# The moving operand of the MLP matmuls, read in turn from two halves

## Chip, cores and metric

One core of one Trainium2 chip runs the whole program. The metric is the device time of one execution in microseconds (us). The kernel before took 1102.36 us (median of three runs, 1100.85 to 1103.11). The profile is of one further execution on the same kind of chip.

## What is computed

Inputs are q, k, v of shape (4, 8, 576, 64), a scalar tau, and four weight matrices that arrive as 8-byte floats. Three stages follow each other; the tokens are 4 x 576 = 2304 and the model width is 512.

```python
scores = q @ k.T / 8
keep   = scores >= max(scores) - tau            # the rest counts as -1e9
x      = softmax(scores over keep) @ v          # -> 2304 x 512
g1     = relu(x @ w1i) ** 2                     # 2304 x 2048
x2     = g1 @ w1o                               # 2304 x 512
h      = x2 @ w2i                               # 2304 x 2048
out    = (h * tanh(log1p(exp(min(h, 20))))) @ w2o
```

## The kernel before

The kernel does not issue its work in the order of its loops. Every piece of work is an `op` with the engines that may do it, a cost for each, and the buffers that it reads and writes. `Plan.order` then simulates the engines with those costs, and the instructions are issued in the order of the simulated starts. The costs are constants in the source: a group of twelve matmuls of an MLP product has `T: 1.41`, a group of six wide ones `T: 1.39`, readers of PSUM `A: 0.48` on ScalarE and `V: 0.6` or `0.66` on VectorE. There is no hand-written order of the MLP work beside this.

The MLP work is cut into nine blocks of 256 tokens. TensorE works on float32 data in its float32r form: each product is the sum of three matmuls, high x high, high x low and low x high, where high is the value as rounded to float32r and low the rest (`passes`).

- **Layer 1, up (`first_part`, `mlp_in`)**: for each of eight slices j of 256 hidden units, two halves f of 128; for each, four chunks c of the model width and three passes. The stationary operand is a 128 x 128 piece of the weights, the moving operand is `x` with 256 columns, one for each token of the block. So it is 24 matmuls of 256 columns for each j, into the PSUM tile `h`.
- **Layer 1, down (`down` in `first_part`)**: the stationary operand is a piece of `w1o`, the moving operand is the 256 tokens of `gh` or `gl`: 24 matmuls of 256 columns for each j, into `acc`.
- **Layer 2, up (`second`, `mlp_in`)**: as in layer 1, 16 groups of 12 matmuls with 256 columns for each block, into halves of `s0`, `s1`, `h` or `small`.
- **Layer 2, down (`down` in `second`)**: here the tokens are the stationary operand (128 of them) and the weights move, with 512 columns: 24 matmuls for each of the four quarters of a block, into `acc`.

Before the change each moving operand is one run of neighbouring 4-byte elements: `r(c)` in `mlp_in` and `z()[:, f, :]` in the two `down`. A piece of PSUM is read by `relu` (L1072) and `evac` (L1106) in layer 1, by `exp` (L1123), `add` (L1182), `gate` (L1195) and `evac` (L1217) in layer 2; each of these reads 512 neighbouring elements and writes 512 neighbouring elements to SBUF. All matmuls are issued by one helper, `mm`, at L379, and stand in the profile under that line. A row such as `h<-xh,wi0l` has the output first, then the moving and the stationary tile.

Attention for the first tokens runs alone; from about 140 us on the first MLP layer runs beside attention, and from about 690 us on the second layer runs by itself.

Of the kernel before, what the change touches and what calls it, by code (L numbers as in the profile page):

```python
# [11 lines left out]
F32 = mybir.dt.float32  # L12
# [292 lines left out]
def attention_moe_moe_kernel(ctx: ExitStack, tc: tile.TileContext, q, k, v, tau, w1i, w1o, w2i, w2o, out):  # L305
# [688 lines left out]
    def mlp_in(layer, j, f, ph, col, x, due):  # L994
        wi = W[layer, 0, j]

        def fn(e):
# [5 lines left out]
        op({"T": 1.41}, fn, r=[wi[0], wi[1], *x[0].bufs, *x[1].bufs],  # L1003
           w=[ph.buf if isinstance(ph, Half) else ph], due=due)

    class View:


# [2 lines left out]

        def __call__(self, c):
            n = 4 // len(self.bufs)
            return self.bufs[c // n]()[:, c % n, :]

    def x_first(n, due):
        xh, xo = sbuf("xh", [128, 4, 256], F32R), sbuf("xo", [128, 4, 256], F32R)
        o = pbuf(rot("s0", "s1"), [128, 1024])
        for t in range(2):
            for g in range(2):  # L1020
                xl = sbuf(rot("xl0", "xl1", "xl2"), [128, 256], F32)
                dma(lambda e, xl=xl, t=t, g=g: e.dma_start(out=xl(), in_=x_dr[n]()[:, t, 256 * g:256 * g + 256]),
                    r=[x_dr[n]], w=[xl], due=due - 4, mb=0.13)

                def turn(e, o=o, xl=xl, z=512 * t + 256 * g):
                    for c in (0, 128):
                        nc.tensor.transpose(o()[:, z + c:z + c + 128], xl()[:, c:c + 128], ident)  # L1027

                op({"T": 0.17}, turn, r=[xl, K], w=[o], due=due - 0.5)

            def part(y, t=t):
                return y()[:, :, 128 * t:128 * t + 128]

            def src(o=o, t=t):
                return o()[:, 512 * t:512 * t + 512].rearrange("p (c n) -> p c n", c=4)

            def hi(e, src=src, part=part):
                if e == "A":
                    nc.scalar.activation(out=part(xh), in_=src(), func=AF.Copy)
                else:  # L1040
                    nc.vector.tensor_copy(out=part(xh), in_=src())

            def lo(e, src=src, part=part):
                nc.vector.tensor_tensor(out=part(xo), in0=src(), in1=f32(part(xh)), op=ALU.subtract)

            op({"A": 0.52, "V": 0.6}, hi, r=[o], w=[xh], due=due - 0.4 - URG)
            op({"V": 0.6}, lo, r=[o, xh], w=[xo], due=due - 0.3 - URG)
        return View([xh]), View([xo])

    def flat(t):  # L1050
        return t().rearrange("p f n -> p (f n)")

    def first(n):
        lent.discard("acc")
# [6 lines left out]
    def first_part(n, j, x, acc):  # L1061
        d = due_f(n, j)
        ph = pbuf("h", [128, 512])
        for f in range(2):
            mlp_in(0, j, f, ph, 256 * f, x, d + 0.1 * f)
        gh, gl = (sbuf(rot(f"{a}0", f"{a}1"), [128, 2, 256], F32R) for a in ("gh", "gl"))

        r = sbuf("r", [128, 512], F32)

        def relu(e, ph=ph, r=r):  # L1070
            if e == "A":
                nc.scalar.activation(out=r(), in_=ph(), func=AF.Relu)  # L1072
            else:
                nc.vector.tensor_scalar(out=r(), in0=ph(), scalar1=0.0, scalar2=None, op0=ALU.max)

        def square(e, r=r):
            if e == "A":
                nc.scalar.activation(out=r(), in_=r(), func=AF.Square)  # L1078
            else:
                VEC[e].tensor_tensor(out=r(), in0=r(), in1=r(), op=ALU.mult)  # L1080

        op({"A": 0.48, "V": 0.66}, relu, r=[ph], w=[r], due=d + 0.3 - URG + O_RELU)
        op({"A": 0.52, "P": 1.04, "V": 0.6}, square, x=[r], due=d + 0.4 + O_SQ, two=True)
        to_hi(r, gh, flat, d + 0.5 + O_SQ)
        to_lo(r, gh, gl, flat, d + 0.6 + O_SQ)
        wo = W[0, 1, j]
        for f in range(2):
            def down(e, j=j, f=f, wo=wo, gh=gh, gl=gl, acc=acc):
                for dt in range(4):
                    a = acc[0]()[:, 256 * dt:256 * dt + 256]  # L1090
                    for i, (l, z) in enumerate(passes(wo, (gh, gl))):
                        mm(a, l()[:, f, 128 * dt:128 * dt + 128], z()[:, f, :],
                           j == 0 and f == 0 and dt % 2 == 0 and i == 0,
                           j == 7 and f == 1 and dt % 2 == 1 and i == 2)

            first_ = j == 0 and f == 0
            op({"T": 1.41}, down, r=[wo[0], wo[1], gh, gl], w=acc if first_ else (),
               x=() if first_ else acc, due=d + 5.5 + O_DN + 0.1 * f)
        if j == NJ - 1:
            for h in range(2):  # L1100
                st = sbuf(rot("stg0", "stg1"), [128, 512], F32)

                def evac(e, h=h, st=st, acc=acc):
                    a = acc[0]()[:, 512 * h:512 * h + 512]
                    if e == "A":
                        nc.scalar.activation(out=st(), in_=a, func=AF.Copy)  # L1106
                    else:
                        nc.vector.tensor_copy(out=st(), in_=a)

                op({"A": 0.48, "V": 0.66}, evac, r=acc, w=[st], due=due_f(n, 7) + 6)  # L1110
                dma(lambda e, n=n, h=h, st=st: e.dma_start(out=x2_dr[n][h](), in_=st()),
                    r=[st], w=[x2_dr[n][h]], due=due_f(n, 7) + 7, mb=0.26)

    def second():
# [10 lines left out]
        for i, n in enumerate((*range(NB - 2), NB - 1, NB - 2)):  # L1125
# [1 line left out]
            hs, os_ = [], []  # L1127
            sets = (("f0", "f1", "e1", "nat0"), ("nat1", "KT0", "KT1", "V0"))[i % 2]
            for g in range(2):
                xr = sbuf(rot("V1", "hl0"), [128, 2, 256], F32)  # L1130
                dma(lambda e, n=n, g=g, xr=xr: e.dma_start(
                    out=xr().rearrange("p c n -> p (c n)"), in_=x2_dr[n][g]()),
                    r=[x2_dr[n][g]], w=[xr], due=blkd - 12, mb=0.26)
                xh, xo = sbuf(sets[2 * g], [128, 2, 256], F32R), sbuf(sets[2 * g + 1], [128, 2, 256], F32R)

                def flat2(t):
                    return t().rearrange("p c n -> p (c n)")

                def hi(e, xr=xr, xh=xh):
                    if e == "A":  # L1140
                        nc.scalar.activation(out=xh(), in_=xr(), func=AF.Copy)
                    elif e == "P":
                        nc.gpsimd.tensor_scalar(out=xh(), in0=xr(), scalar1=1.0, scalar2=0.0, op0=ALU.mult, op1=ALU.add)
                    else:
                        nc.vector.tensor_copy(out=xh(), in_=xr())

                def lo(e, xr=xr, xh=xh, xo=xo):
                    VEC[e].tensor_tensor(out=xo(), in0=xr(), in1=f32(xh()), op=ALU.subtract)

                op({"A": 0.52, "V": 0.34, "P": 0.66}, hi, r=[xr], w=[xh], due=blkd - 6, two=True)  # L1150
                op({"V": 0.6, "P": 1.24}, lo, r=[xr, xh], w=[xo], due=blkd - 5, two=True)
                hs.append(xh)
                os_.append(xo)
            x = View(hs), View(os_)
            acc = [pbuf("acc", [128, 1024])]
            for qd in range(4):
# [3 lines left out]
                    mlp_in(1, 2 * qd + f // 2, f % 2, ph[f // 2], 256 * (f % 2), x, d + 0.1 * f)  # L1160
                es = [sbuf(rot("pt2", "hl1", "f2", "Q0", "Q1"), [128, 512], F32) for _ in range(2)]
                gs = [sbuf(rot("r", "e0"), [128, 512], F32) for _ in range(2)]
                ghs = [sbuf(rot("gh0", "gh1", "pt0"), [128, 2, 256], F32R) for _ in range(2)]
                gls = [sbuf(rot("gl0", "gl1", "pt1"), [128, 2, 256], F32R) for _ in range(2)]
                for z in range(2):
                    def exp(e, z=z, ph=ph, ex=es[z]):
                        act(AF.Exp, "ln", ex(), ph[z]())

                    def cap(e, ex=es[z]):
                        nc.vector.tensor_scalar(out=ex(), in0=ex(), scalar1=E20, scalar2=None, op0=ALU.min)  # L1170
# [9 lines left out]
                for z in range(2):  # L1180
                    def add(e, z=z, ph=ph, ex=es[z]):
                        nc.vector.scalar_tensor_tensor(  # L1182
                            out=ex(), in0=ph[z](), scalar=20.0, in1=ex(), op0=ALU.min, op1=ALU.add
                        )

                    op({"V": 0.6}, add, r=[ph[z].buf], x=[es[z]], due=d + 0.8)
# [5 lines left out]
                op({"A": 1.04}, sig, x=es, due=d + 0.9, tab=("sig",))  # L1192
                for z in range(2):
                    def gate(e, z=z, ph=ph, ex=es[z], g=gs[z]):
                        nc.vector.tensor_tensor(out=g(), in0=ph[z](), in1=ex(), op=ALU.mult)  # L1195

                    op({"V": 0.6}, gate, r=[ph[z].buf, es[z]], w=[gs[z]], due=d + 1.0)
                    to_hi(gs[z], ghs[z], flat, d + 1.1)
# [1 line left out]
                for f in range(4):  # L1200
# [3 lines left out]
                    def down(e, f=f, qd=qd, wo=wo, g2=g2, acc=acc):  # L1204
                        for t in range(2):
                            for i, (z, l) in enumerate(passes(wo, g2)):
                                mm(acc[0]()[:, 512 * t:512 * t + 512], l()[:, f % 2, 128 * t:128 * t + 128], z()[:, f % 2, :],
                                   qd == 0 and f == 0 and i == 0, qd == 3 and f == 3 and i == 2)

                    first_ = qd == 0 and f == 0  # L1210
# [2 lines left out]
            ob = sbuf(rot("xh", "xo"), [128, 2, 512], F32)  # L1213
            for t in range(2):
                def evac(e, t=t, ob=ob, acc=acc):
                    if e == "A":
                        nc.scalar.activation(out=ob()[:, t, :], in_=acc[0]()[:, 512 * t:512 * t + 512], func=AF.Copy)  # L1217
                    else:
                        nc.vector.tensor_copy(out=ob()[:, t, :], in_=acc[0]()[:, 512 * t:512 * t + 512])

                op({"A": 0.48, "V": 0.66}, evac, r=acc, w=[ob], due=blk[NB + i + 1] + 6)

# [96 lines left out]
```

## Time and profile before

| what | value |
|---|---|
| time, median of three runs | 1102.36 us |
| span of the profiled execution | 1101.5 us |
| granted TensorE clock, mean over the span | 0.982 |
| instructions | 23735 |
| matmuls / weight loads in the trace | 9364 / 9364 |

The span is the time from the first to the last instruction of the profiled execution; it lies 0.9 us under the median of the runs. TensorE has two rows: PE, its matmuls, and PEld, its weight loads, which run beside the matmuls. Matmuls overlap each other, so the time that one costs in a dense stream is the distance from its start to the start of the next, not the duration in its row. [...]

### The profile page before, as it was taken

Reading aid. Unit: us, or ns where it says so; the run is one execution under the profiler, and the core shown is the slowest. Engines: PE = TensorE matmul, PEld = TensorE weight load, DVE = VectorE, ACT = ScalarE, POOL = GpSimd, SP = SyncE. Lnnn points to the kernel's source line nnn. Section 1 sums busy time; section 2 is a strip of 40 time slices with the busy share of each in tenths; the row PEclk is TensorE's granted clock in tenths of the full one; section 3 lists DMA queues with packets and bytes.
Section 4 is the critical chain, followed back from the end, with each engine's and each line's share of the span. In section 5 each row is a group of like instructions: output and inputs, shape, how many; then the busy total and the mean of one; then the engine's idle time right before and its main releaser. Section 6 shows DMA issues by size and latency. Waiting matters only on the chain.

```text
span 1101.5 us, 23735 instructions
## 1 busy us (share of the span) xinstructions
PE 1058.0 (96%) x9364; PEld 946.4 (86%) x9364; DVE 745.8 (68%) x1768; ACT 787.4 (71%) x1309; POOL 39.8 (4%) x38
## 2 busy tenths in 40 slices
PE   6788899899999999999999999999999999999998
PEld 4566598788898888898999999998899889989896
DVE  5889999999888998769664149854544445443352
ACT  6789798777777778667575369967766667676584
POOL 1231012000000000000000000000000000000000
PEclk9898889999999999999999999999999999999999
DMA  9535447888968988875664024310100101000000
GB/s 258 165 116 148 127 112 154 158 171 164 178 125 156 169 163 161 153 148 110 140 228 142 20 78 153 116 40 20 39 20 20 39 1 39 21 20 20 1 20 20
DMA packets 246416, 113.75 MB, mean 103 GB/s; under 512 B 211104, under 2 KB 228000, under 8 KB 246304
## 3 DMA queue, kind: packets, MB, share of 16 engines
q1 hardware_dynamic: 246016, 111.71, 43.8%
q8 instruction: 73, 1.20, 0.4%
q10 hardware_dynamic: 288, 0.52, 0.1%
q14 instruction: 39, 0.32, 0.1%
HBM read 58.33 MB, written 14.16 MB: 66 GB/s over the span
## 4 chain that ended last, share of the span: by engine, by line
PE 68%; DVE 6%; DMA 5%; ACT 2%; issue 2%; SPq 1%; DVEq 0%; ACTq 0%
PE acc L379 31%; PE h L379 16%; PE s L379 14%; PE small L379 6%; DMA pt<-hl 3%; DMA pt<-area 2%; DVE e L777 1%; DVE area L743 1%; DVE hl L806 1%; DVE area L806 1%; DMA area<-in_q_dram 1%; PE s L1027 0%; ACT e L766 0%; ACT area L801 0%; ACT hl L801 0%
## 5 line engine op out<-in xcount | busy, mean ns | idle before, releaser
L379 PE MATMUL s<-KT,area 64*128 64x64 f16 (+6 forms) x880 | 89.9, 327 | 4.8 <-ACT area L684 2.5
L508 DVE TENSOR_TENSOR gl<-r,gh 128x512 fp32r<-128x512 f32 x87 | 60.0, 690 | 47.7 <-ACT gh L498 46.2
L766 ACT ACTIVATE e<-area,m 128x576 f32<-128x576 f32 x100 | 75.6, 768 | 22.3 <-DVE area L743 9.5
L1119 ACT ACT_TABLE_LOAD x70 | 89.8, 1283 | 1.2
L743 DVE TENSOR_SCALAR_CACHE_REDUCE area<-s,c 128x576 f32<-128x576 f32 x100 | 79.5, 812 | 12.1 <-PE s L379 11.4
L777 DVE SCALAR_TENSOR_TENSOR e<-area,n,e 128x576 f32<-128x576 f32 x100 | 80.1, 813 | 5.5 <-ACT e L766 4.3
L1072 ACT ACTIVATE r<-h 128x512 f32<-128x512 f32 x72 | 42.8, 595 | 44.9 <-PE h L379 40.0
L806 DVE TENSOR_TENSOR hl<-e,hl 128x512 f16<-128x512 f32 (+1 forms) x142 | 64.5, 466 | 14.3 <-ACT hl L801 14.0
L498 ACT ACTIVATE gh<-r 128x512 fp32r<-128x512 f32 x90 | 56.6, 629 | 22.1 <-PE acc L379 19.9
L379 PE MATMUL small<-V,pt 128*128 128x64 f16 (+1 forms) x1680 | 64.1, 195 | 4.6 <-DMA pt<-hl 2.4
L1170 DVE TENSOR_SCALAR area<-area 128x512 f32<-128x512 f32 x37 | 15.8, 426 | 77.9 <-ACT area L1123 77.8
L379 PEld LDWEIGHTS <-pt 128*128 128x128 f16 (+1 forms) x1680 | 54.7, 101 | 15.2 <-issue 6.9
L801 ACT ACTIVATE hl<-e 128x576 f16<-128x576 f32 x74 | 50.2, 680 | 22.4 <-DMA pt<-hl 10.6
L508 DVE TENSOR_TENSOR gl<-e,gh 128x512 fp32r<-128x512 f32 x36 | 24.8, 690 | 39.8 <-ACT gh L498 39.7
L1123 ACT ACTIVATE area<-s 128x512 f32<-128x512 f32 x24 | 14.3, 598 | 46.1 <-PE s L379 46.1
L498 ACT ACTIVATE gh<-e 128x512 fp32r<-128x512 f32 x36 | 22.6, 629 | 33.7 <-PE acc L379 33.6
L1123 ACT ACTIVATE area<-area 128x512 f32<-128x512 f32 x74 | 46.3, 630 | 0.5
L1078 ACT ACTIVATE r<-r 128x512 f32<-128x512 f32 x72 | 45.3, 629 | 1.2
L379 PEld LDWEIGHTS <-area 64*128 64x128 f16 (+1 forms) x720 | 23.5, 97 | 21.0 <-issue 1.8
L379 PEld LDWEIGHTS s<-KT,area 64*128 64x128 f32 (+1 forms) x160 | 19.5, 209 | 19.4 <-issue 10.8
L806 DVE TENSOR_TENSOR area<-e,area 128x512 f16<-128x512 f32 (+1 forms) x67 | 30.5, 460 | 5.7 <-ACT area L801 5.7
L1195 DVE TENSOR_TENSOR r<-s,area 128x512 f32<-128x512 f32 x23 | 15.9, 691 | 27.1 <-ACT area L1123 27.1
(755 smaller groups left out, 4062.9 us busy)
## 6 DMA issues: line engine op xcount, KB each, us to landing
area<-in_moe_w_in_dram SPq DMA_DIRECT2D x22, 512.0 KB, 4.1
area<-in_moe_w_out_dram SPq DMA_DIRECT2D x22, 512.0 KB, 4.1
xl<-xdr SPq DMA_DIRECT2D x36, 128.0 KB, 2.6
x2dr<-stg SPq DMA_DIRECT2D x18, 256.0 KB, 4.0
xdr<-xs SPq DMA_DIRECT2D x32, 128.0 KB, 2.3
f<-in_v_dram SPq DMA_DIRECT2D x12, 256.0 KB, 3.0
f<-in_k_dram SPq DMA_DIRECT2D x22, 128.0 KB, 3.1
area<-in_q_dram SPq DMA_DIRECT2D x20, 128.0 KB, 2.8
```

The costliest lines, as they stand in the source:

```text
L379: nc.tensor.matmul(o, l, r, start=start, stop=stop, skip_group_check=True)
L498: nc.scalar.activation(out=o, in_=i, func=AF.Copy)
L508: VEC[e].tensor_tensor(out=part(lo), in0=src(), in1=f32(part(hi)), op=ALU.subtract)
L743: nc.vector.tensor_scalar(out=sc(), in0=s()[:, 0:576], scalar1=c()[:, 3:4], scalar2=None, op0=ALU.mult, op1=ALU.min, accum_out=m()[:, i:i ...
L766: lambda e: nc.scalar.activation(out=ex(), in_=sc(), func=AF.Exp, bias=m()[:, i:i + 1], scale=-1.0),
L777: nc.vector.scalar_tensor_tensor(out=ex(), in0=sc(), scalar=nt()[:, i:i + 1], in1=ex(), op0=ALU.is_le, op1=ALU.mult, accum_out=l()[:, 0, u ...
L801: nc.scalar.activation(out=hl()[:, 0:576], in_=ex(), func=AF.Copy)
L806: VEC[e].tensor_tensor(out=hl()[:, a:a + n], in0=ex()[:, z:z + n], in1=hl()[:, z:z + n], op=ALU.subtract)
L1072: nc.scalar.activation(out=r(), in_=ph(), func=AF.Relu)
L1078: nc.scalar.activation(out=r(), in_=r(), func=AF.Square)
L1119: nc.scalar.preload_act_table_set({"ln": "natural_log_exp_and_others", "sig": "sigmoid_and_others"}[table])
L1123: nc.scalar.activation(out=out, in_=in_, func=func, **kw)
```

## The change

Each tile that is a moving operand gets another order of its elements, or another order in which they are read. The tiles of tokens become two halves of 128 tokens, `[128, a, f, 128]` with a the half, instead of `[128, f, 256]`. A matmul then reads column 0 from half 0, column 0 from half 1, column 1 from half 0, and so on: neighbouring columns of the stream lie 2048 bytes apart (layer 1 up) or 1024 bytes apart (the other three products), and every second step goes back. For layer 2 down the weights keep their place, and their 512 columns are read in turn from two halves of 256 columns. The number of matmuls, their column counts and the PSUM places that they write stay as they are, and they write neighbouring columns of PSUM. Since the columns there are now mixed, the six readers of PSUM read every second element (a step of 8 bytes), first one half and then the other, and write neighbouring elements. The stationary operand of layer 2 down is still a run of 128 elements, taken at another offset. No cost and no parameter of the planner is changed, and no `op` is added or taken away.

```diff
+    def turned_out(t):
+        return t.rearrange("p (k a) -> p a k", a=2)
+
+    def halves(t):
+        return t.rearrange("p (a k) -> p a k", a=2)
...
         def __call__(self, c):
             n = 4 // len(self.bufs)
-            return self.bufs[c // n]()[:, c % n, :]
+            return self.bufs[c // n]()[:, :, c % n, :].rearrange("p a b -> p b a")
...
-        xh, xo = sbuf("xh", [128, 4, 256], F32R), sbuf("xo", [128, 4, 256], F32R)
+        xh, xo = sbuf("xh", [128, 2, 4, 128], F32R), sbuf("xo", [128, 2, 4, 128], F32R)
...
-                return y()[:, :, 128 * t:128 * t + 128]
+                return y()[:, t]
...
             if e == "A":
-                nc.scalar.activation(out=r(), in_=ph(), func=AF.Relu)
+                nc.scalar.activation(out=halves(r()), in_=turned_out(ph()), func=AF.Relu)
...
-                        mm(a, l()[:, f, 128 * dt:128 * dt + 128], z()[:, f, :],
+                        mm(a, l()[:, f, 128 * dt:128 * dt + 128], z()[:, :, f, :].rearrange("p a b -> p b a"),
...
-                    a = acc[0]()[:, 512 * h:512 * h + 512]
+                    a = turned_out(acc[0]()[:, 512 * h:512 * h + 512])
                     if e == "A":
-                        nc.scalar.activation(out=st(), in_=a, func=AF.Copy)
+                        nc.scalar.activation(out=halves(st()), in_=a, func=AF.Copy)
...
-                        act(AF.Exp, "ln", ex(), ph[z]())
+                        act(AF.Exp, "ln", halves(ex()), turned_out(ph[z]()))
...
-                            out=ex(), in0=ph[z](), scalar=20.0, in1=ex(), op0=ALU.min, op1=ALU.add
+                            out=halves(ex()), in0=turned_out(ph[z]()), scalar=20.0, in1=halves(ex()),
+                            op0=ALU.min, op1=ALU.add,
...
-                        nc.vector.tensor_tensor(out=g(), in0=ph[z](), in1=ex(), op=ALU.mult)
+                        nc.vector.tensor_tensor(
+                            out=halves(g()), in0=turned_out(ph[z]()), in1=halves(ex()), op=ALU.mult)
...
-                                mm(acc[0]()[:, 512 * t:512 * t + 512], l()[:, f % 2, 128 * t:128 * t + 128], z()[:, f % 2, :],
+                                mm(acc[0]()[:, 512 * t:512 * t + 512], l()[:, t, f % 2, :],
+                                   z()[:, f % 2, :].rearrange("p (a b) -> p b a", a=2),
...
+                    o, i = halves(ob()[:, t, :]), turned_out(acc[0]()[:, 512 * t:512 * t + 512])
                     if e == "A":
-                        nc.scalar.activation(out=ob()[:, t, :], in_=acc[0]()[:, 512 * t:512 * t + 512], func=AF.Copy)
+                        nc.scalar.activation(out=o, in_=i, func=AF.Copy)
```

## Rows read from the trace of the kernel before

**Rows 1.** Page, part 1: busy us (share of the span) and instructions of each engine.

```profile
PE 1058.0 (96%) x9364; PEld 946.4 (86%) x9364; DVE 745.8 (68%) x1768; ACT 787.4 (71%) x1309; POOL 39.8 (4%) x38
```

**Rows 2.** Windows: stretch, length, busy of PE, PEld, DVE, ACT, POOL, then clock, DMA share, GB/s.

```profile
0.00:212.65 212.65, 181.13 (x1550) 140.78 (x1552) 186.06 (x480) 174.88 (x326) 34.01 (x32) 0.91 0.60 154
212.65:300.00 87.35, 83.40 (x1052) 74.22 (x1049) 78.63 (x230) 65.86 (x115) 1.07 (x2) 1.00 0.87 171
300.00:500.00 200.00, 197.86 (x2388) 178.73 (x2385) 169.35 (x493) 145.22 (x250) 4.74 (x4) 1.00 0.81 151
500.00:700.00 200.00, 199.60 (x1866) 195.29 (x1866) 124.45 (x253) 129.34 (x223) 0.00 (x0) 1.00 0.47 130
700.00:1100.00 400.00, 396.05 (x2520) 357.34 (x2519) 187.27 (x317) 272.06 (x399) 0.00 (x0) 1.00 0.07 25
```

**Rows 3.** Waits of TensorE from 300 to 1095 us: total us, times, longest.

```profile
PE small L379 <- DMA pt<-hl: 1.6, 4, 0.6
PE h L379 <- DVE r L1195: 0.5, 1, 0.5
```

**Rows 4.** Waits of ScalarE from 300 to 1095 us: total us, times, longest.

```profile
ACT gh L498 <- PE acc L379: 52.3, 31, 4.7
ACT area L1123 <- PE s L379: 46.1, 15, 6.5
ACT r L1072 <- PE h L379: 38.5, 27, 4.2
```

**Rows 5.** Chain in order of time, 240 to 1101 us: start, us, what, matmuls in it.

```profile
731.51 11.30 PE s L379 x96
...
1033.48 11.17 PE acc L379 x48
```

**Rows 6.** Windows: one stretch in which nearly every matmul has 256 columns.

```profile
625.00:675.00 50.00, 50.00 (x423) 50.00 (x423) 27.02 (x46) 33.63 (x62) 0.00 (x0) 1.00 0.25 78
```

**Rows 7.** Timeline of TensorE, a quick stretch: start, duration; sixteen matmuls from first row to last.

```profile
600.06 0.28 PE L379 MATMUL h<-xo,wi1h 128*128 128x256 f32 x1
...
601.88 0.28 PE L379 MATMUL h<-xh,wi1l 128*128 128x256 f32 x1
```

**Rows 8.** Timeline of TensorE, a slow stretch: nine matmuls from first row to last.

```profile
630.25 0.28 PE L379 MATMUL acc<-gh,wo3h 128*128 128x256 f32 x1
...
631.34 0.28 PE L379 MATMUL acc<-gh,wo4h 128*128 128x256 f32 x1
```

**Rows 9.** Timeline of TensorE, scores in float16: from row to row 512 and 64 columns.

```profile
335.93 0.63 PE L379 MATMUL s<-KT,area 64*64 64x512 f16 x6
...
336.18 0.41 PE L379 MATMUL s<-KT,area 64*64 64x512 f16 x4
```

**Rows 10.** Windows: a stretch at the lower clock.

```profile
139.00:141.00 2.00, 2.00 (x11) 2.00 (x11) 2.00 (x5) 1.46 (x3) 1.97 (x2) 0.50 0.03 8
```

**Rows 11.** Timeline of TensorE in that stretch: six matmuls from first row to last.

```profile
139.17 0.41 PE L379 MATMUL h<-xo,wi0h 128*128 128x256 f32 x1
...
140.45 0.41 PE L379 MATMUL h<-xo,wi0h 128*128 128x256 f32 x1
```

**Rows 12.** Groups by form: count, then busy us, mean ns; idle before, and releaser.

```profile
L1072 ACT ACTIVATE r<-h 128x512 f32<-128x512 f32 x72 | 42.8, 595 | 44.9 <-PE h L379 40.0 <-DVE gl L508 3.8 <-DVE hl L806 0.7
L1078 ACT ACTIVATE r<-r 128x512 f32<-128x512 f32 x72 | 45.3, 629 | 1.2
L457 ACT ACTIVATE area<-area 128x512 int32<-128x512 uint32 x44 | 30.0, 681 | 0.0
L857 ACT ACTIVATE wo4l<-h 128x512 f32<-128x512 f32 x18 | 10.8, 601 | 1.1 <-PE small L379 1.1
L857 ACT ACTIVATE wo4l<-small 128x128 f32<-128x128 f32 x18 | 5.1, 283 | 0.4 <-PE small L907 0.4
L464 DVE SCALAR_TENSOR_TENSOR KT<-KT,area 128x512 int32<-128x512 int32 x10 | 6.9, 692 | 1.7 <-ACT area L457 1.4
L1182 DVE SCALAR_TENSOR_TENSOR area<-s,area 128x512 f32<-128x512 f32 x24 | 16.5, 688 | 7.1 <-ACT area L1123 7.0
```

More of the change, by code (lines that the diff above doesn't have):

```diff
@@ L1050, in flat @@
     def flat(t):
-        return t().rearrange("p f n -> p (f n)")
+        return t().rearrange("p a f b -> p (a f b)")
     def first(n):
@@ L1065, in first_part @@
             mlp_in(0, j, f, ph, 256 * f, x, d + 0.1 * f)
-        gh, gl = (sbuf(rot(f"{a}0", f"{a}1"), [128, 2, 256], F32R) for a in ("gh", "gl"))
+        gh, gl = (sbuf(rot(f"{a}0", f"{a}1"), [128, 2, 2, 128], F32R) for a in ("gh", "gl"))
         r = sbuf("r", [128, 512], F32)
@@ L1071, in relu @@
             if e == "A":
-                nc.scalar.activation(out=r(), in_=ph(), func=AF.Relu)
+                nc.scalar.activation(out=halves(r()), in_=turned_out(ph()), func=AF.Relu)
             else:
-                nc.vector.tensor_scalar(out=r(), in0=ph(), scalar1=0.0, scalar2=None, op0=ALU.max)
+                nc.vector.tensor_scalar(
+                    out=halves(r()), in0=turned_out(ph()), scalar1=0.0, scalar2=None, op0=ALU.max)
         def square(e, r=r):
@@ L1103, in evac @@
                 def evac(e, h=h, st=st, acc=acc):
-                    a = acc[0]()[:, 512 * h:512 * h + 512]
+                    a = turned_out(acc[0]()[:, 512 * h:512 * h + 512])
                     if e == "A":
-                        nc.scalar.activation(out=st(), in_=a, func=AF.Copy)
+                        nc.scalar.activation(out=halves(st()), in_=a, func=AF.Copy)
                     else:
-                        nc.vector.tensor_copy(out=st(), in_=a)
+                        nc.vector.tensor_copy(out=halves(st()), in_=a)
                 op({"A": 0.48, "V": 0.66}, evac, r=acc, w=[st], due=due_f(n, 7) + 6)
@@ L1129, in second @@
             for g in range(2):
-                xr = sbuf(rot("V1", "hl0"), [128, 2, 256], F32)
+                xr = sbuf(rot("V1", "hl0"), [128, 2, 2, 128], F32)
                 dma(lambda e, n=n, g=g, xr=xr: e.dma_start(
-                    out=xr().rearrange("p c n -> p (c n)"), in_=x2_dr[n][g]()),
+                    out=flat(xr), in_=x2_dr[n][g]()),
                     r=[x2_dr[n][g]], w=[xr], due=blkd - 12, mb=0.26)
-                xh, xo = sbuf(sets[2 * g], [128, 2, 256], F32R), sbuf(sets[2 * g + 1], [128, 2, 256], F32R)
-                def flat2(t):
-                    return t().rearrange("p c n -> p (c n)")
+                xh, xo = (sbuf(sets[2 * g + i], [128, 2, 2, 128], F32R) for i in range(2))
                 def hi(e, xr=xr, xh=xh):
@@ L1162, in second @@
                 gs = [sbuf(rot("r", "e0"), [128, 512], F32) for _ in range(2)]
-                ghs = [sbuf(rot("gh0", "gh1", "pt0"), [128, 2, 256], F32R) for _ in range(2)]
-                gls = [sbuf(rot("gl0", "gl1", "pt1"), [128, 2, 256], F32R) for _ in range(2)]
+                ghs = [sbuf(rot("gh0", "gh1", "pt0"), [128, 2, 2, 128], F32R) for _ in range(2)]
+                gls = [sbuf(rot("gl0", "gl1", "pt1"), [128, 2, 2, 128], F32R) for _ in range(2)]
                 for z in range(2):
                     def exp(e, z=z, ph=ph, ex=es[z]):
-                        act(AF.Exp, "ln", ex(), ph[z]())
+                        act(AF.Exp, "ln", halves(ex()), turned_out(ph[z]()))
                     def cap(e, ex=es[z]):
@@ L1215, in evac @@
                 def evac(e, t=t, ob=ob, acc=acc):
+                    o, i = halves(ob()[:, t, :]), turned_out(acc[0]()[:, 512 * t:512 * t + 512])
                     if e == "A":
-                        nc.scalar.activation(out=ob()[:, t, :], in_=acc[0]()[:, 512 * t:512 * t + 512], func=AF.Copy)
+                        nc.scalar.activation(out=o, in_=i, func=AF.Copy)
                     else:
-                        nc.vector.tensor_copy(out=ob()[:, t, :], in_=acc[0]()[:, 512 * t:512 * t + 512])
+                        nc.vector.tensor_copy(out=o, in_=i)
                 op({"A": 0.48, "V": 0.66}, evac, r=acc, w=[ob], due=blk[NB + i + 1] + 6)
```

## The prediction, made before the changed kernel ran

> **What bounds the kernel now.** I read the share of busy time first, then cut it into stretches, then looked at who waits for whom, and last at the distance between two matmuls. TensorE is busy for 96% of the span [rows 1], but that is a mean. By stretches it is 85% up to 212.65 us, 95% up to 300 us, and 99 to 100% after it, at clock 1.00, while VectorE goes from 85% down to 47% and ScalarE stays near 70% [rows 2]. From 300 us on the waits of TensorE are nothing: the longest sum is 1.6 us [rows 3]. The other way round ScalarE waits 52.3, 46.1 and 38.5 us for TensorE at three of its lines [rows 4]. So from 300 us to the end the time is the number of matmuls times the distance between their starts, and nothing but that distance can move it much.
>
> The distance is the thing to see. A stretch of the chain with 96 matmuls of 256 columns takes 11.30 us, 117.7 ns each; 48 of 512 columns take 11.17 us, 232.7 ns each [rows 5]. A stretch of the first layer gives 50.00 us / 423 = 118.2 ns [rows 6]. [...] It depends on which tiles meet: one stretch runs at (601.88 - 600.06) / 16 = 113.8 ns [rows 7], another at (631.34 - 630.25) / 9 = 121.1 ns [rows 8], of the same shape. [...]
>
> **The change part by part.** It adds and removes no instruction, no wait, no DMA and no planner cost, so the issue order of every queue stays. What changes is how long three kinds of instructions take.
>
> *Moving reads.* By the source there are 9 x 8 x 48 + 9 x 16 x 12 = 5184 matmuls of 256 columns and 9 x 4 x 24 = 864 of 512. The trace has no moving operand that jumps, so the new price is bounded from both sides. Low end: no loss, 106.7 and 213.3 ns, which saves 11.3 x 5184 = 58.6 us and 19 x 864 = 16.4 us, 75 us. High end: every column comes at the pace of the lower clock, 213.3 ns [rows 11] and twice that, which adds 95 x 5184 = 492 us and 194 x 864 = 168 us, 660 us. Nearest row for a stream whose supply is not the limit: float16, 0.434 ns a column [rows 9], that is 111.1 and 222.2 ns. I take that: two streams that are read in turn give each of them twice the time for its next piece, as half the bytes per column do. It saves 6.9 x 5184 = 35.8 us (from 118.0) and 9.8 x 864 = 8.5 us (from 232), 44.3 us. Not all of it counts. The first block of layer 1 lies before 212.65 us, where TensorE is idle for 15% [rows 2]; I give nothing for its 384 matmuls (2.6 us) and half for the next 384 (1.3 us). 44.3 - 3.9 = 40.4 us. The next limit is VectorE: from 212.65 to 500 us it is busy 248 of 287 us [rows 2], so a gain of 4% on TensorE (some 12 us there) still fits.
>
> [...]
>
> *Readers of PSUM.* 90 reads on ScalarE in layer 1 (72 `relu`, 18 `evac`, 595 ns each [rows 12]), and in layer 2 72 `exp`, 72 `add`, 72 `gate` and 18 `evac`. They now step by 8 bytes. Low end: nothing; on VectorE an operand in SBUF with that step (L464) takes 692 ns against 688 for neighbouring ones [rows 12]. High end: each element costs twice; 384 elements more cost 601 - 283 = 318 ns, 0.83 ns each, so 512 would cost 0.42 us more. Nearest row: the ScalarE read of SBUF with an 8-byte step, 681 ns against 629 [rows 12], 0.05 us. I take 0.05 us, about 9 us in all on ScalarE. Its cover is the waiting for TensorE [rows 4]. Even the high end, 90 x 0.42 = 38 us on ScalarE in each layer, fits under 272 of 400 us [rows 2] in layer 2, so I cost it at nothing; without the cover it would be those 9 us.
>
> *Writes of `xh`, `xo`, `gh`, `gl` and the stationary read at another offset.* Same element counts, still runs of 128 or more. Nothing either way.
>
> The sum: 1101.5 - 40.4 = 1061.1 us of span, and 0.9 us for the distance of the span to the median of the runs: 1062 us.
>
> **Rivals.**
>
> 1. *A smaller gain.* The loss stays as a floor and only the bad meetings of tiles go, so every matmul runs like the best stretch, 113.8 ns [rows 7], and 512 columns in the same ratio, 224 ns. It saves 4.2 x 5184 + 8.5 x 864 = 29 us, less 2.4 us for the first blocks: about 1075 us. For it: the 113.8 is steady over sixteen matmuls. This belongs to the forecast's case.
>
> [...]
>
> 3. *Somewhat slower.* The moving stream now touches two places at a time and meets the weight loads, which run beside it for 86% of the span [rows 1], more often. At the price of the bad stretch, 121.1 ns [rows 8], and 238 ns in the same ratio, it is 3.1 x 5184 + 6 x 864 = 21 us: 1123 us; twice as many meetings give 1144 us.
>
> 4. *It does not do what it says.* The loss has nothing to do with the order of the columns (it comes with float32r itself, or with the weight loads alone): 1102 us.
>
> **How the numbers follow.** Forecast and the smaller gain 0.55, rival 2 0.20, rival 3 0.13, rival 4 0.12. [...] The forecast's own range is 1034 us (no loss at all, 1102.4 - 68 with the first blocks taken out) to 1092 us (a quarter of the gain). The range that leaves out 2 in 10 goes from 1034 up to 1144 us, the upper price of rival 3, and leaves out rival 2 alone. Faster by over 0.2% (about what a measurement of this kernel can tell from no change): 0.55. Within 0.2%: 0.12. Slower: 0.33.
>
> **What would show it.** In the profile after: the distance between matmuls of 256 columns in the stretch of rows 6 and in the chain. Near 111 ns and the same in all stretches, the forecast is right; 113 to 114, the smaller gain; 118, rival 4; over 121, rival 3; near 213 at clock 1.00, rival 2. The 512-column matmuls should move in the same ratio, since the change treats them alike; if only one shape moves, the reason is the distance between the halves or the weight loads, and not the turn. ScalarE reads of PSUM near 0.65 us confirm the price of the step; near 1.0 us they would be the high end, still covered. If the distance falls and the time does not, the gain was lost between 212 and 500 us to VectorE. The prediction is wrong if the distance does not fall below 117 ns.

## The result and the profile after

The changed kernel takes 1072.73 us (median of four runs, 1072.09 to 1072.95) against 1102.41 us before: a ratio of 0.9737, 95% interval 0.9723 to 0.9751, 29.7 us less. The forecast was 1062 us, 40 us less. Its profiled execution has a span of 1070.3 us, 31.2 us under the span before.

The page's first part, against [rows 1]: TensorE loses 45 us of busy time; VectorE gains 3.6 us and ScalarE 7.8 us, though the change gives them no new work.

```profile
PE 1013.1 (95%) x9364; PEld 914.4 (85%) x9364; DVE 749.4 (70%) x1768; ACT 795.2 (74%) x1309; POOL 40.0 (4%) x38
```

The windows after, with the columns of [rows 2]:

```profile
0.00:212.65 212.65, 178.35 (x1591) 136.68 (x1592) 187.51 (x481) 177.65 (x327) 34.25 (x32) 0.94 0.62 154
212.65:300.00 87.35, 81.22 (x1018) 72.19 (x1017) 77.62 (x230) 64.72 (x114) 1.07 (x2) 0.98 0.91 170
300.00:500.00 200.00, 193.46 (x2402) 174.66 (x2399) 171.12 (x498) 145.25 (x249) 4.71 (x4) 1.00 0.85 153
500.00:700.00 200.00, 195.98 (x1917) 190.82 (x1915) 132.78 (x260) 142.99 (x235) 0.00 (x0) 1.00 0.49 131
700.00:1070.00 370.00, 364.09 (x2448) 340.03 (x2448) 180.33 (x304) 264.59 (x387) 0.00 (x0) 1.00 0.08 25
```

From 300 to 500 us TensorE now works 193.46 of 200 us, where it had 197.86, and issues 2402 matmuls there against 2388. It has become quicker and waits more; hardly any work was pulled forward.

The chain in order of time, against [rows 5]: a stretch of 256 columns and one of 512. 96 matmuls take 10.72 us, 111.7 ns each (117.7 before); 48 take 10.36 us, 215.8 ns each (232.7 before).

```profile
722.88 10.72 PE s L379 x96
...
1006.30 10.36 PE acc L379 x48
```

A stretch of the first layer, against [rows 6]: 35.00 us / 314 = 111.5 ns.

```profile
625.00:660.00 35.00, 35.00 (x314) 34.85 (x314) 20.39 (x34) 25.86 (x48) 0.00 (x0) 1.00 0.27 86
```

Taken over all pairs of neighbouring starts within a product, the 256-column matmuls are at 111.6 to 111.7 ns in all three products that have them, nearly all between 111 and 112, where before they lay between 112 and 125 with means of 117.9 to 118.7. The 512-column ones went from 232.1 to 215.9. What the read in turn removed is nearly all of the spread, and 6 to 7 ns of some 118 for 256 columns and 16.2 ns of 232.1 for 512.

Waits of TensorE from 290 to 1065 us, against [rows 3]: the transposes of the attention weights by DMA (`pt<-hl`) are waited for longest, 5.1 us against 1.6.

```profile
PE small L379 <- DMA pt<-hl: 5.1, 8, 1.2
PE h L379 <- DVE r L1200: 2.0, 1, 2.0
PE h L379 <- ACT r L1078: 1.5, 2, 0.8
```

The readers of PSUM with an 8-byte step, against [rows 12]: `relu` (L1072, now L1078) 594 ns where it took 595, `add` (L1182, now L1186) 686 against 688. The step cost nothing there. But a read that the change does not touch has become slower. The conversion of the weights on ScalarE reads SBUF with an 8-byte step (L457), 799 ns where it took 681; this line alone is 5.2 of ScalarE's 7.8 us.

```profile
L1078 ACT ACTIVATE r<-h 128x512 f32<-128x512 f32 x72 | 42.8, 594 | 36.7 <-PE h L379 30.2 <-DVE gl L508 5.7 <-DVE hl L464 0.8
L457 ACT ACTIVATE area<-area 128x512 int32<-128x512 uint32 x44 | 35.2, 799 | 0.0
...
L1186 DVE SCALAR_TENSOR_TENSOR area<-s,area 128x512 f32<-128x512 f32 x24 | 16.5, 686 | 6.8 <-ACT area L1130 6.8
```

Where the time came from is seen by three marks of TensorE's timeline: the first matmul of layer 1, the last group of attention's value products, and the first matmul of layer 2 into `h` (a first group of layer 2, into `small`, runs just before it).

```profile
134.99 0.58 PE L379 MATMUL h<-xh,wi0h 128*128 128x256 f32 x1 [1.66 <-ACT xh L1045]
...
550.08 1.48 PE L379 MATMUL small<-V,pt 128*128 128x64 f16 x42
...
678.88 0.49 PE L379 MATMUL h<-f,wi0h 128*128 128x256 f32 x2 [0.65 <-ACT r L1078]
```

The same marks in the runs that keep the order of the work, as lengths of the stages between them in us (from the timelines of one execution each; before has its marks at 137.30, 554.11 and 686.94):

| stage | before | after | layer 1 only | layer 2 only | before, light DMA | after, light DMA | after, light mask |
|---|---|---|---|---|---|---|---|
| attention alone | 137.3 | 135.0 | 132.2 | 131.9 | 136.8 | 134.9 | 134.1 |
| layer 1 beside attention | 416.8 | 415.1 | 414.2 | 416.4 | 410.9 | 402.8 | 408.5 |
| rest of layer 1 | 132.8 | 128.8 | 129.1 | 132.8 | 132.8 | 127.6 | 128.7 |
| layer 2 | 414.6 | 391.4 | 414.2 | 391.3 | 414.5 | 391.5 | 392.5 |

Of the 31.2 us, 23.2 come from layer 2, 4.0 from the rest of layer 1, and 1.7 from the long middle stage, which holds some 2370 of the 3456 matmuls of layer 1. The 2.3 us of the first stage, which has no MLP matmul, are its own spread: it is between 131.9 and 137.3 us in these runs, and goes with the granted clock, which from 0 to 130 us was 0.89 before (137.3 us) and 0.92 after (135.0 us). So 28.9 us lie in the stages that have the change. The rest of layer 1 holds 1080 of the matmuls, some 7.2 us of quicker reads by the distances above, of which 4.0 arrive: TensorE, which shows no wait there before, now waits 1.5 us for ScalarE (`r`) and 0.8 us for VectorE (`gl`).

### The profile page after: what moved, and what is told of

It is laid out like the page before. It is cut to its first block, busy times and chain, and to the rows that moved or that the text cites. A ratio compares the mean times of both kernels' runs of the same rounds, so it can differ in the third digit from the quotient of the medians.

```text
span 1070.3 us, 23743 instructions
## 1 busy us (share of the span) xinstructions
PE 1013.1 (95%) x9364; PEld 914.4 (85%) x9364; DVE 749.4 (70%) x1768; ACT 795.2 (74%) x1309; POOL 40.0 (4%) x38
## 5 line engine op out<-in xcount | busy, mean ns | idle before, releaser
L743 DVE TENSOR_SCALAR_CACHE_REDUCE area<-s,c 128x576 f32<-128x576 f32 x100 | 79.4, 811 | 10.7 <-PE s L379 10.2
L1078 ACT ACTIVATE r<-h 128x512 f32<-128x512 f32 x72 | 42.8, 594 | 36.7 <-PE h L379 30.2
L498 ACT ACTIVATE gh<-r 128x512 fp32r<-128x512 f32 x90 | 56.6, 629 | 16.2 <-PE acc L379 13.6
L379 PEld LDWEIGHTS <-area 64*128 64x128 f16 (+1 forms) x720 | 24.5, 97 | 22.2 <-issue 3.8
L457 ACT ACTIVATE area<-area 128x512 int32<-128x512 uint32 x44 | 35.2, 799 | 0.0
```

The lines of the kernel that those rows point to most:

```text
L379: nc.tensor.matmul(o, l, r, start=start, stop=stop, skip_group_check=True)
L498: nc.scalar.activation(out=o, in_=i, func=AF.Copy)
L743: nc.vector.tensor_scalar(out=sc(), in0=s()[:, 0:576], scalar1=c()[:, 3:4], scalar2=None, op0=ALU.mult, op1=ALU.min, accum_out=m()[:, i:i ...
L1078: nc.scalar.activation(out=halves(r()), in_=turned_out(ph()), func=AF.Relu)
```

## The experiments

**What a way of reading costs.** This kernel leaves out all of the reference. It issues bursts of matmuls that differ only in the pattern of the moving operand.

```diff
+ def mv(kind, i, t, cols=256):        # t: float32r data in SBUF, b: one of four offsets
+     run:    t[:, b:b + cols]
+     half d: t[:, b:b + 2*d] as "p (a k) -> p k a", a=2      # two halves, d elements apart
+     step s: every s-th element
+     four d: as half, with a=4
+     piece n: n neighbours of one half, then n of the other
+     near n:  within one run, from two neighbouring pieces of n elements in turn
+ for i in range(96):
+     matmul(psum, W[:, 128*(i%8):128*(i%8)+m], mv(kind, i, X, cols), start=True, stop=True)
```

> A kernel that computes nothing of the reference: 96 matmuls of 128x128 by 256 (or 512) columns one after the other for each way of reading the moving operand, the same weights each time. Read: distance between starts. Theory A (the moving operand is supplied by one place of SBUF at a time, and two places in turn hide the loss): a run of neighbours 113 to 118 ns, halves in turn 512, 1024 or 2048 bytes apart 111 to 112 ns, with 512 columns 232 and 216 ns; with only 32 stationary columns the run stays at 113 or more; steps of 16 and 64 bytes not slower than the run. Theory B (the run meets the weight loads, which are 128 columns each): with 32 stationary columns the run falls to 109 to 111 ns as well. [...] The rest of 111.7 against 106.7 ns: if weight loads of 128 columns set it, halves with 32 stationary columns fall to 107 to 109 ns; if it is a cost of each matmul they stay at 111.7. float16: 107 to 110 ns for run and halves alike.

Each window below goes from the start of a burst's ninth matmul to the start of its last, 87 distances. In order: run, halves 512, 1024 and 2048 bytes apart, steps of 8, 16 and 64 bytes, four in turn, pieces of 2, 4 and 16, pieces of 8 neighbours in turn (`near 8`), then a run and halves with only 32 stationary columns, run and halves with 512 columns.

```profile
45.10:55.54 10.44, 10.44 (x89) 10.44 (x88) 0.00 (x0) 0.00 (x0) 0.00 (x0) 1.00 0.01 2
56.55:66.27 9.72, 9.72 (x90) 9.72 (x88) 0.00 (x0) 0.00 (x0) 0.00 (x0) 1.00 0.01 2
67.27:76.99 9.72, 9.72 (x90) 9.72 (x88) 0.00 (x0) 0.00 (x0) 0.00 (x0) 1.00 0.01 2
77.99:87.71 9.72, 9.72 (x90) 9.72 (x88) 0.00 (x0) 0.00 (x0) 0.00 (x0) 1.00 0.00 0
89.62:109.34 19.72, 19.72 (x88) 18.01 (x87) 0.00 (x0) 0.00 (x0) 0.00 (x0) 1.00 0.00 1
111.44:131.74 20.30, 20.30 (x89) 18.07 (x88) 0.00 (x0) 0.00 (x0) 0.00 (x0) 1.00 0.00 1
133.73:152.86 19.13, 19.13 (x88) 17.86 (x87) 0.00 (x0) 0.00 (x0) 0.00 (x0) 1.00 0.00 1
154.24:166.71 12.47, 12.47 (x90) 12.47 (x89) 0.00 (x0) 0.00 (x0) 0.00 (x0) 1.00 0.00 0
168.18:182.68 14.50, 14.50 (x89) 14.50 (x88) 0.00 (x0) 0.00 (x0) 0.00 (x0) 1.00 0.00 1
183.88:194.90 11.02, 11.02 (x90) 11.02 (x88) 0.00 (x0) 0.00 (x0) 0.00 (x0) 1.00 0.01 1
195.99:206.43 10.44, 10.44 (x90) 10.44 (x89) 0.00 (x0) 0.00 (x0) 0.00 (x0) 1.00 0.01 2
207.44:217.16 9.72, 9.72 (x90) 9.72 (x89) 0.00 (x0) 0.00 (x0) 0.00 (x0) 1.00 0.00 0
...
239.63:249.49 9.86, 9.86 (x89) 9.38 (x88) 0.00 (x0) 0.00 (x0) 0.00 (x0) 1.00 0.01 2
250.48:259.98 9.50, 9.50 (x90) 9.49 (x89) 0.00 (x0) 0.00 (x0) 0.00 (x0) 1.00 0.00 0
261.94:281.67 19.73, 19.73 (x89) 16.33 (x87) 0.00 (x0) 0.00 (x0) 0.00 (x0) 1.00 0.00 1
283.62:302.40 18.78, 18.78 (x89) 16.44 (x87) 0.00 (x0) 0.00 (x0) 0.00 (x0) 1.00 0.00 1
```

| moving operand | ns for each matmul |
|---|---|
| run | 120.0 |
| halves 512, 1024, 2048 bytes apart | 111.7 each |
| pieces of 8, 16, 32 neighbours in turn, within one run (`near`) | 111.7 each |
| step of 8 / 16 / 64 bytes | 226.7 / 233.3 / 219.9 |
| four in turn, 1024 bytes apart | 143.3 |
| pieces of 2 / 4 / 16 from each half | 166.7 / 126.7 / 120.0 |
| 32 stationary columns: run / halves | 113.3 / 109.2 |
| 512 columns: run / halves | 226.8 / 215.9 |
| float16: run / halves 512 bytes apart | 109.2 / 243.3 |
| float16: run of 512 columns | 215.8 |

So the gain of the change is a matter of the pattern alone: 120.0 to 111.7 ns, in a kernel with nothing else running. The distance between the two places made no difference, from 2048 bytes down to neighbouring pieces of 32 bytes: 111.7 ns each. Each theory got a part. A run takes less with narrow weights (113.3 against 120.0), as theory B has it, and yet stays above halves (109.2), as theory A has it: a part of the time goes with the order of the moving read and a part with the width of the stationary operand. Read in turn, the two widths are 2.5 ns apart (111.7 and 109.2), as runs 6.7. That it is the weight loads that the read meets is argued and not shown. Steps of 16 and 64 bytes are near half the pace (233.3 and 219.9 ns), where theory A had them no slower than the run. A step of 8 bytes is as slow (226.7), and halves, which jump at every column, are among the fastest (111.7).

**Which columns lie together.** That asked for a second measurement, with the same bursts and other patterns.

```diff
+ halfstep s: two halves in turn, with a step of s elements inside each
+ near 2: order 0 2 1 3 | 4 6 5 7 ...      near 4: order 0 4 1 5 2 6 3 7 | ...
```

> [...] float16: if pairs of neighbours are fetched together, pieces of 2 and of 4 in turn are near 109 ns and steps of 4 bytes or halves near 220 to 245; if not, the pieces are slow too. Weight loads: a run with 32 stationary columns 113.3 as before, with 64 between 113 and 120; halves with 64 at 109.

The windows, 87 distances each: run, `near 2`, `near 4`, halves with steps of 8 and of 16 bytes inside.

```profile
54.92:65.36 10.44, 10.44 (x89) 10.44 (x88) 0.00 (x0) 0.00 (x0) 0.00 (x0) 1.00 0.01 2
66.44:76.88 10.44, 10.44 (x89) 10.44 (x88) 0.00 (x0) 0.00 (x0) 0.00 (x0) 1.00 0.01 2
77.90:87.61 9.71, 9.71 (x89) 9.71 (x88) 0.00 (x0) 0.00 (x0) 0.00 (x0) 1.00 0.00 0
88.68:99.12 10.44, 10.44 (x90) 10.44 (x89) 0.00 (x0) 0.00 (x0) 0.00 (x0) 1.00 0.01 2
101.03:120.75 19.72, 19.72 (x88) 18.06 (x87) 0.00 (x0) 0.00 (x0) 0.00 (x0) 1.00 0.00 1
```

These are 120.0, 120.0, 111.7, 120.0 and 226.7 ns. Most of the float32r times of both measurements, all with 128 stationary columns and 256 moving ones, go with a count: take every second column of the stream, and count how many of these come in a row from the same 16 bytes. In a run, in pieces of 16, in `near 2` and in halves with a step of 8 bytes inside there are two: 120.0 ns each. In halves and in `near 4`, 8, 16 and 32 there are four: 111.7 each. With a step of 8, 16 or 64 bytes, and in halves with a step of 16 bytes inside, there is one: 219.9 to 233.3. The 16 bytes are read from these times as well: by 8 bytes a run (120.0) and a step of 8 bytes (226.7) would both count one, by 32 a run (120.0) and `near 4` (111.7) would both count four. Pieces of 2 and 4 and four in turn (166.7, 126.7 and 143.3 ns) do not go with the count. It describes times and no more; how the chip reads is not seen. For float16 the guess in the expectation fell: pieces of 2 take 136.7 ns and not 109, a step of 4 bytes 113.3 and not 220 (pieces of 4 take 113.3). Nor does a read in turn cost float16 anything as such: `near 2`, neighbours in the order 0 2 1 3, takes 109.2 ns there like a run. Halves 512 bytes apart take 243.3, where in float32r they take 111.7: the count does not hold for float16, and why they are slow stays open. In this run the burst with 32 stationary columns took 117.8 ns where it took 113.3 before, and with 64 it took 113.3; what the width of the stationary operand does to a run is not told by these numbers either.

**One layer at a time.** The changed kernel with the runs put back in one of the layers. The store between the layers is written in the order that the next one reads.

```diff
 layer 2 only (of several like it):
-                        mm(a, l()[:, f, ...], z()[:, :, f, :].rearrange("p a b -> p b a"),
+                        mm(a, l()[:, f, ...], z()[:, f, :],
...
 layer 1 only (of several like it):
-                                   z()[:, f % 2, :].rearrange("p (a b) -> p b a", a=2),
+                                   z()[:, f % 2, :],
...
```

> The change in layer 2 alone; layer 1 reads runs. Layer 2 runs by itself, so its whole gain should reach the end: 1728 x 6.3 ns + 864 x 16.2 ns = 25 us, 1077 to 1080 us. If the gain of the full change (29.7 us) came mostly from layer 1, this would stay above 1088.

Measured 1076.39 us, ratio 0.9779 (0.9752 to 0.9806) to before, 24.5 us under the kernel before on the same chip and 0.6 us beyond the quick end of what was expected. Layer 2 falls from 414.6 to 391.3 us, as in the full change, and the middle stage stays at 416.4. Layer 1 reads runs here, and the slow read of the weights' conversion is gone with it: from 550 to 670 us L457 takes 672 ns (675 before), but 807 with layer 1 alone changed (809 in the changed kernel). So the slower read goes with layer 1 read in turn; what in it does so is not shown. The line of that stretch with layer 2 alone changed, then with layer 1 alone:

```profile
L457 ACT ACTIVATE area<-area 128x512 int32<-128x512 uint32 x20 | 13.4, 672 | 0.0
...
L457 ACT ACTIVATE area<-area 128x512 int32<-128x512 uint32 x21 | 16.9, 807 | 0.0
```

> The change in layer 1 alone; layer 2 reads runs. Theory 'TensorE bounds the stage beside attention': 3456 x 6.6 ns = 23 us, about 1080 us. Theory 'something else bounds it until attention ends near 520 us': only the 1344 matmuls after that count, 8 to 9 us, 1092 to 1096 us.

Measured 1091.78 us, ratio 0.9916 (0.9891 to 0.9940), 9.1 us under the kernel before on the same chip, 0.2 us beyond the quick end of the second theory's range. The second theory is the one that fits: of the 11.7 us between the two profiled executions, 3.7 come from the rest of layer 1, 2.6 from the middle stage, and 5.1 from the first stage, where the change has nothing. Its matmuls are at 111.7 ns all through; the speed is there and the time is not.

**What bounds the middle stage.** Two kernels that take work from the suspects, both on the changed kernel. The first leaves the low part of the attention weights out of the result.

```diff
-        transpose(pt, hl, [hl], [pt], due + 4 + O_HL)
+        transpose(lambda: pt()[:, 0:5], lambda: hl()[:, 0:640], [hl], [pt], due + 4 + O_HL)
-                    mm(o()..., pt()[:, i, sl], V()[:, t, 0:64], i == 0, i == 8)
+                    mm(o()..., pt()[:, i % 5, sl], V()[:, t, 0:64], i == 0, i == 8)
```

> The changed kernel; each DMA transpose of attention weights moves 5 blocks of 128 columns in place of 9, and TensorE reads the first blocks again in place of the other four (the low part of the attention weights is left out of the result); all instructions of the other engines stay. Theory 'DMA sets the pace beside attention' (DMA share 0.87 to 0.93 there): 8 to 14 us faster than the changed kernel's 1072.7. Theory 'VectorE does' or 'the order does': under 4 us.

> The changed kernel; the masking of attention weights (144 instructions on VectorE of 0.81 us) works on 64 of 576 columns, which leaves the mask out for the rest, and 1.0 is added to the sums so that they stay finite; nothing else. Theory 'VectorE sets the pace beside attention' (busy 0.91 to 0.93 in two stretches): some 75 us of VectorE go, 8 us or more come off 1072.7. Theory 'DMA' or 'the order': under 4 us.

The second edit, of which the diff shows the mask alone:

```diff
-                out=ex(), in0=sc(), scalar=nt()[:, i:i + 1], in1=ex(), op0=ALU.is_le, op1=ALU.mult,
+                out=ex()[:, 0:64], in0=sc()[:, 0:64], scalar=nt()[:, i:i + 1], in1=ex()[:, 0:64],
+                op0=ALU.is_le, op1=ALU.mult,
...
```

The light DMA gives 1060.26 us, ratio 0.9629 (0.9596 to 0.9663), 12 us under the changed kernel; the middle stage falls from 415.1 to 402.8 us. The light mask gives 1064.41 us, ratio 0.9666 (0.9641 to 0.9690), 8 us under it, with a middle stage of 408.5 us and 65 us less work on VectorE. Each theory has the gain that it gave beforehand, and each had given the other under 4 us: neither is the one bound. Both suspects pace the stage, the transposes more. The some 2370 matmuls of layer 1 in this stage are worth 15.8 us by their distances, and 1.7 arrive; a lighter transpose gives 12.3 us more, a lighter mask 6.6. That the change has slowed the transposes themselves is not seen: from issue to landing they take 3.4 us before and after.

Was it so before the change? The same edit on the kernel before:

> The lighter DMA transposes (5 blocks in place of 9, low part of the attention weights left out of the result, TensorE's matmuls as many as before) on the kernel before. Theory 'the stage beside attention was paced by the transposes already, TensorE only looked full': it gains there about as much as the changed kernel did (10 us between 247 and 521 us, 12 us in all: 1088 to 1092 us). Theory 'TensorE bound the stage before, and the change handed it over to DMA and VectorE': under 4 us there, 1096 us or more.

Measured 1095.01 us, ratio 0.9938 (0.9917 to 0.9960); the middle stage falls by 5.9 us, from 416.8 to 410.9, and not by 12.3. The windows from 247 to 507 us, of before, after, before with the light DMA, and after with it:

```profile
247.00:507.00 260.00, 254.94 (x3055) 230.58 (x3055) 223.26 (x647) 190.84 (x328) 5.49 (x5) 1.00 0.82 156
```

```profile
247.00:507.00 260.00, 250.52 (x3102) 226.17 (x3100) 224.48 (x653) 191.68 (x330) 5.47 (x5) 0.99 0.86 157
```

```profile
247.00:507.00 260.00, 258.73 (x3125) 234.16 (x3124) 226.92 (x656) 191.38 (x330) 5.50 (x5) 1.00 0.62 121
```

```profile
247.00:507.00 260.00, 257.70 (x3220) 232.07 (x3219) 233.75 (x681) 197.46 (x340) 5.48 (x5) 1.00 0.63 123
```

The numbers lie between the two theories. Alone, quicker matmuls give 1.7 us in this stage and lighter transposes 5.9; together they give 14.0, nearly twice the sum. (Kernels that differ in layer 2 alone are 0.4 and 0.9 us apart here, so the 1.7 is small but the 14.0 is clear of that.) So before the change two bounds stood side by side, TensorE and the work of attention on VectorE and in the transposes, and taking one away shows the other. A lighter mask on the kernel before, and lighter work on ScalarE, were not run; what part each has in the second bound stays open.

**The planner's costs.** The changed kernel with the costs of the MLP groups set to what was measured, in both layers, in layer 2 alone, and half of the way.

```diff
-        op({"T": 1.41}, ...        op({"T": 1.39}, ...
+        op({"T": 1.34}, ...        op({"T": 1.30}, ...      # replan
+        op({"T": 1.34 if layer else 1.41}, ...    op({"T": 1.30}, ...   # replan_l2
+        op({"T": 1.38}, ...        op({"T": 1.35}, ...      # replan_half
```

> The changed kernel with the planner's costs of MLP groups set to the measured ones (1.34 and 1.30 us in place of 1.41 and 1.39). Theory 'the order was laid out for slower matmuls, and the gain beside attention is lost to that order': up to 14 us come back, 1059 to 1068 us. Theory 'another resource bounds the stage': no gain, 1070 us or, since the whole order is drawn anew, somewhat more (to 1085).

> The changed kernel with the planner's costs set to the measured ones in layer 2 alone. Theory 'any new draw of the order loses against the tuned one': 1074 to 1082 us. Theory 'the costs of layer 1 were what misled the first redrawn order': 1066 to 1072 us.

> The changed kernel with planner's costs half of the way (1.38 and 1.35). Theory 'any new draw loses': 1074 to 1082 us. Theory 'right costs help and only the draw was bad': 1062 to 1072 us.

Measured 1079.16 us, ratio 0.9796 (0.9766 to 0.9826); 1070.67 us, 0.9730 (0.9712 to 0.9747); 1074.28 us, 0.9763 (0.9741 to 0.9786). The right costs everywhere are the worst of the three. The best of them is not told apart from the changed kernel (0.9723 to 0.9751). The order is drawn anew each time, and in these three draws better costs did not buy a better order; the middle stage stays at 413 to 415 us in all three, so the gain lost there does not come back this way. No version here that computes the whole result beats the changed kernel beyond its interval.

## Why the prediction was right, and where it was not

- **What bounds the kernel.** Right for layer 2, where 23.2 us came out of 24.9 us of quicker matmuls (1728 x 6.3 ns + 864 x 16.2 ns). Wrong for the middle stage. "From 300 us on the waits of TensorE are nothing" [rows 3] was read as "nothing but that distance can move it", but an engine that hardly waits can still have another bound right behind it. This is the step that was mis-sized: "Not all of it counts" took off 3.9 us, and the runs took off 18.8 (47.7 us of quicker matmuls by the measured distances, 5184 x 6.5 ns + 864 x 16.2 ns, against 28.9 us in the stages that have them): 14 of them in the middle stage, 3 in the rest of layer 1, 1.7 in layer 2. That "a gain of 4% on TensorE (some 12 us there) still fits" beside VectorE's 248 of 287 us [rows 2] looked at a busy sum; lighter transposes and a lighter mask show a second bound behind TensorE, which was 98% busy from 212.65 to 500 us. The last part of the prediction had named the place for such a loss, between 212 and 500 us, and VectorE; the transposes weigh more, and they are not in it.
- **Moving reads.** The bursts show that the order in which the moving operand is read changes the distance by itself (120.0 to 111.7 ns); by what mechanism is not shown. The size was taken from float16 [rows 9], as a stream "whose supply is not the limit", which no run shows: 111.1 ns, measured 111.7, and 222.2, measured 215.9. The second was 6 ns too high, 5 us over 864 matmuls. A plain run in float16 takes 109.2 and 215.8 ns, so the 0.434 ns a column of that row, two matmuls in times given to 0.01 us, was not the price of float16 either; that 111.1 met 111.7 is in part luck. No run shows the low end of the range, 106.7 and 213.3 ns at clock 1.00: 106.7 is half of the (140.45 - 139.17) / 6 = 213.3 ns that 256 columns took at granted clock 0.50 [rows 10] [rows 11], an estimate, and the quickest bursts took 109.2 ns for 256 columns and 215.8 for 512. The gain of the matmuls was put 3.4 us too low and the discount from it 14.9 us too low; with 2.3 us less in the first stage, and 2.4 us between span and median where 0.9 was taken, the sum came out 10.7 us too low.
- **Two streams "give each of them twice the time for its next piece, as half the bytes per column do".** The likeness to float16 was wrong as a reason: float16 itself falls to under half the pace when it is read from halves 512 bytes apart (243.3 ns against 109.2).
- **Readers of PSUM.** Costed at nothing for their cover; they cost nothing in themselves, 594 against 595 ns, where 0.05 us was taken. ScalarE's busy time still rose by 7.8 us, near the 9 us of that sum, but by the conversion of the weights, which the prediction does not have: the nearness is luck.
- **Rivals.** The smaller gain gave 1075 us, nearer to the 1072.73 than the forecast, by another way: not a floor of 113.8 ns, but a distance of 111.7 whose gain arrives only in part. Near 213 ns at clock 1.00, the mark of rival 2, is what steps of 8, 16 and 64 bytes come to (219.9 to 233.3 ns), and not the read in turn (111.7). The sign rested on a choice that no row of before could settle, the pattern having no example there; a burst of a few microseconds would have settled it.

## What to carry to other kernels

Where a dense stream of float32r matmuls of 256 columns is at 118 to 120 ns at granted clock 1.00, look at the order in which its columns are read: two places read in turn, even 16 bytes apart (`near 4`), took 7% off (120.0 to 111.7 ns), at no cost for readers of PSUM that put the columns back with an 8-byte step (`relu` 594 ns against 595). Look at the other engines' reads too: ScalarE's reads of SBUF with an 8-byte step became a sixth slower beside it (681 to 799 ns). Measure the pattern alone before a kernel is rebuilt for it, with the data type that it will have: halves 512 bytes apart more than double the time in float16 (109.2 to 243.3 ns). And before a gain on a full engine is counted, take work from its neighbours in a trial: here an engine that was 98% busy had a second bound right behind it.

## What the runs showed of the hardware

- float32r, 256 columns, clock 1.00: 111.7 ns from two places in turn, 120.0 from a run, 220 to 233 with a step of 8, 16 or 64 bytes. With 32 or 64 stationary columns, two places in turn take 109.2 ns.
- float32r, 256 columns in a run, granted clock 0.50 [rows 10]: 213.3 ns [rows 11].
- ScalarE's read of SBUF with an 8-byte step (L457) took 681 ns beside runs and 799 beside reads in turn; VectorE's (L464) 692 and 752.
- float16 in turn from two halves takes 243.3 ns against 109.2 for a run; in turn from neighbouring pairs (`near 2`) 109.2. In the first measurement the burst after it, with steps of 16 bytes, ran at granted clock 0.50, 39.29 us / 87 = 451.6 ns for each matmul; before the clock fell, TensorE had done that slow burst of halves at clock 1.00. In the second measurement the same burst was followed by a run at clock 1.00. The windows: float16 run, halves and steps, then `near 2` of the second measurement.

```profile
303.50:313.00 9.50, 9.50 (x90) 8.51 (x87) 0.00 (x0) 0.00 (x0) 0.00 (x0) 1.00 0.01 2
315.05:336.22 21.17, 21.17 (x88) 8.52 (x87) 0.00 (x0) 0.00 (x0) 0.00 (x0) 1.00 0.00 0
340.06:379.35 39.29, 39.29 (x88) 10.93 (x87) 0.00 (x0) 0.00 (x0) 0.00 (x0) 0.50 0.00 0
...
263.96:273.45 9.49, 9.49 (x89) 8.51 (x87) 0.00 (x0) 0.00 (x0) 0.00 (x0) 1.00 0.01 2
```
